# A scan and two mixture-of-experts layers: the first tile table in one run on VectorE

## The chip, the core and the metric

The kernel runs on one core of a Trainium2 chip. The metric is the time of the whole program in microseconds of the device; a run's profile also gives the span from the first to the last instruction. TensorE does the matrix products, VectorE and ScalarE the work on elements, GpSimd the writes to indexed rows, and SyncE and ScalarE issue most of the other transfers.

## The reference

The input is 2 sequences of 5056 tokens with 256 features. A gated scan along each sequence is followed by two layers that send each token to the one expert of eight with the highest logit:

```python
f = lower_bound + (1.0 - lower_bound) * sig        # sig = sigmoid(f_logit)
for t in range(S):
    h = f[:, t] * h + (1.0 - f[:, t]) * x[:, t]
    y[:, t] = h
# layer 1: logits = (y/|y|) @ (emb/|emb|).T / tau; layer 2: logits = x @ w_gate
expert_idx = argmax(logits)
out[mask] = gate_w[mask] * (relu(x[mask] @ w1[e]) @ w2[e])   # for each expert e
```

The 10112 tokens are 79 tiles of 128. w1 is 8 x 256 x 1024 and w2 8 x 1024 x 256 in each layer.

## The kernel before

**Products in half precision.** Each fp32 operand is split into a half-precision part and a remainder (hi and lo), and three products of the parts are summed. So each of the 64 weight blocks (512 KB: layer, w1 or w2, half h of the 1024 hidden features, expert e) is loaded, its hi part is written by ScalarE (`w_hi`, L410), and its lo part, the weight remainder, by VectorE (`w_lo`, L207). For four blocks of the first 16 (`wpe`, numbers 2, 6, 9 and 12) TensorE makes the remainder instead (`w_sub`, L447 and L448) and ScalarE copies it out (`w_sub2`, L456). L207, L211, L212 and L215 are helpers that many steps share.

**Names in rows.** W_0_102 and W_1_103 are the two halves of w1, W_0_104 and W_1_105 those of w2. The weights of the first half are made first; until they are needed, the second halves' memory holds raw weights and the first eight chunks of the input. `ws` is one of three other buffers for raw weights.

**Chunks and groups.** The scan goes over 40 chunks of 256 tokens (two tiles). A chunk is loaded (L488), gated (L495, L501), multiplied (the product, L521 through L207, which reads `xf` and writes `xf`), scanned (two L529), turned by TensorE into `yt` (L578, L580), squared (L595), scaled and split into a row (L618 and L207 `row`). Two chunks make a group q of four tiles: its best expert is found (`lg`, `mx`, `er`, `m`, `oh`), TensorE ranks its tokens among those of their expert (`rank_mm`, L466 and L468, which writes `RK`), VectorE reads the slots (`er<-RK`, `sl`), TensorE moves the counts up (`rank_up`, L473 and L475), and GpSimd puts the rows into the DRAM tensor X at their slots (`p_put`, L714), four transfers a group.

**Tables and units.** After groups 3 and 5 and others `checkpoint` reads the counts and writes a table (`ci`, `ct`, `le`, `tab`) of the tiles of one expert that are full; the first has 9 tiles. SyncE reads the table and loads such a tile turned (`xT`, L837); the load waits for all puts of the table's groups. A unit is one tile and one half h: 24 products with w1 into `hps` (L880), ScalarE's relu (L893), VectorE's remainder `hT<-hps` (L207), and three units later 12 products with w2 into `ops` (L912), which ScalarE copies out (L916). The first 8 tiles go through h = 0 as units 0 to 7 and through h = 1 as units 8 to 15. TensorE's six accumulator buffers are shared by `yt`, `wd`, `hps` and `ops`.

**What sets the order.** A plan gives each step a number and a rank in it; chunk c's steps count from `s0[c]`, which runs from -29 for the first chunk, and for chunk 8 jumps to `hold[1]`; from chunk 10 on `first` sets it. Up to step 17 only SyncE keeps the order of the plan: that of the other engines is made by a scheduler when the program is built, from the plan's priorities. `tc.issue_after(i)` holds instructions in that order behind instruction i.

Of the kernel before, what the change touches and what calls it, by code (L numbers as in the profile page):

```python
# [14 lines left out]
ALU = mybir.AluOpType  # L15
# [46 lines left out]
          'gat': (9, 54),  # L62
          'put': (10, 12),
          'cp': (10, 58)},
 'hold': (8, -9),
 'rates': ((17, 2), (99, 4)),
 'alias': 8,
 'mans': 17,
# [76 lines left out]
def scan_moe_moe_kernel(ctx, tc, xf, emb, cst, tmp, w1a, w2a, w1b, w2b, out, seq, cfg=CFG):  # L145
# [59 lines left out]
    def stt(eng, out, in0, s, in1, op0, op1, **kw):  # L205
        assert eng is V
        return eng.scalar_tensor_tensor(out=out, in0=in0, scalar=s, in1=in1, op0=op0, op1=op1, **kw)  # L207
# [15 lines left out]
    def ins_of(i):  # L223
        return getattr(i, "ins", i)
# [245 lines left out]
    def rank_up(m, oh, g):  # L470
        b = rkb[m][0]
        r = RK[:, b:b + g, :]
        T.matmul(out=r, lhsT=tri16b, rhs=oh[:, 0:g, :], start=False, stop=True, skip_group_check=True)  # L473
        for s in range(1, g):
            T.matmul(out=r[:, 0:g - s, :], lhsT=ones16, rhs=oh[:, s:g, :], start=False, stop=True, skip_group_check=True)  # L475


    ck = {}
    pq = {}
    prev = {}  # L480

    def p_load(c, eng=None):
        g = min(CT, NT - c * CT)
# [25 lines left out]
    def p_scan(c):  # L509
        d = ck[c]  # L510
        n, t = d["g"] * P, d["t"]
        f, y = t[:, 2:4, 0:n], t[:, 0:2, 0:n]
        if p_split(c):
            tt(G, y, f, y, ALU.mult)
            eng = cfg["y1"][c % len(cfg["y1"])]
            if eng == "A":
                A.activation(out=f, in_=f, func=ACTF.Copy, bias=1.0)
            else:
                ts(G if eng == "G" else V, f, f, 1.0, None, ALU.add)
        else:  # L520
            stt(V, y, f, 1.0, y, ALU.subtract, ALU.mult)  # L521
        yield
        a = c * TW
        cuts = [0] + [b - a for b in range(seq, N, seq) if a < b < a + n] + [n]
        for i in range(len(cuts) - 1):
            lo, hi = cuts[i], cuts[i + 1]
            for k in range(2):
                init = 0.0 if (a + lo) % seq == 0 else (t[:, k, lo - 1:lo] if lo else prev["y"][:, k])
                V.tensor_tensor_scan(out=t[:, k, lo:hi], data0=t[:, 2 + k, lo:hi], data1=t[:, k, lo:hi],  # L529
                                     initial=init, op0=ALU.mult, op1=ALU.subtract)  # L530
                yield
        prev["y"] = t[:, 0:2, n - 1:n]
# [157 lines left out]
        p["sl"] = sl  # L690

    def p_up(q):
        rank_up(0, pq[q]["oh"], pq[q]["g"])
        counted[0] += pq[q]["g"]

    def p_gat(q):
        p = pq[q]
        g, row = p["g"], p["row"]
        xv = row[:, :, 512:RW].bitcast(F32)
        G.tensor_copy(out=xv[:, 0:g, 1], in_=tok[:, q * G4:q * G4 + g])  # L700
        se = sm.tile([P, G4, 1], F32, name="se", tag="se")
        V.tensor_reduce(out=se[:, 0:g], in_=p["sh"][:, 0:g], axis=AX.X, op=ALU.add)
        yield
        stt(V, se[:, 0:g, 0], se[:, 0:g, 0], 1e-9, p["sc"][:, 0:g], ALU.add, ALU.mult)
        yield
        V.reciprocal(out=xv[:, 0:g, 0:1], in_=se[:, 0:g])
        yield

    def p_put(q, rows):
# [519 lines left out]
    def wstep(load, hi, lo, lo2):  # L1229
# [7 lines left out]
        if lo is not None:  # L1237
            t = wbuf.pop(lo)
            nlo[0] += 1
            i = nlo[0]  # L1240
            if i in cfg["wpe"]:
                wps[lo] = (w_sub(lo, t), t)
            elif 16 < i <= 32 and tablast:
                with behind(lo, V, tablast[0]):
                    w_lo(lo, t)
                w_done(lo)
            else:
                w_lo(lo, t)
                w_done(lo)
        if hi is not None:  # L1250
            with behind(hi, A):
# [275 lines left out]
```

## Time and profile before

| | us |
|---|---|
| median of 3 runs | 1048.29 (1043.24 to 1054.22) |
| the profiled execution | 1049.57 |
| its span | 1047.8 |
| TensorE busy in the span | 983.6 (94%) |
| VectorE, ScalarE, GpSimd busy | 780.0, 516.2, 428.2 |

The profile is one execution, so its times are compared with its own 1049.57 us, 1.8 us of which lie outside the span. Busy shares are means over the span: the first tenth, in which the scan and the weights are prepared, looks different from the rest.

### The profile page before, as it was taken

Reading aid. Unit: us, or ns where it says so; the run is one execution under the profiler, and the core shown is the slowest. Engines: PE = TensorE matmul, PEld = TensorE weight load, DVE = VectorE, ACT = ScalarE, POOL = GpSimd, SP = SyncE. Lnnn points to the kernel's source line nnn. Section 1 sums busy time; section 2 is a strip of 40 time slices with the busy share of each in tenths; the row PEclk is TensorE's granted clock in tenths of the full one; section 3 lists DMA queues with packets and bytes.
Section 4 is the critical chain, followed back from the end, with each engine's and each line's share of the span. In section 5 each row is a group of like instructions: output and inputs, shape, how many; then the busy total and the mean of one; then the engine's idle time right before and its main releaser. Section 6 shows DMA issues by size and latency. Waiting matters only on the chain.

```text
span 1047.8 us, 33840 instructions
## 1 busy us (share of the span) xinstructions
PE 983.6 (94%) x11795; PEld 859.2 (82%) x11795; DVE 780.0 (74%) x2288; ACT 516.2 (49%) x1266; POOL 428.2 (41%) x686
## 2 busy tenths in 40 slices
PE   5647999998999999999999999999999999999997
PEld 4436899897999899999999888998777777777775
DVE  7878797787888786765448877447777777777775
ACT  6867666555655554665345565443333333333332
POOL 5642447665666565432003550243222222222223
PEclk9967999999999999999999999999999999999999
DMA  9797545887888785965379699652222222221220
GB/s 355 244 328 170 158 93 136 155 163 135 166 161 157 141 150 104 203 200 147 60 181 208 112 212 245 116 104 72 52 52 52 52 52 51 46 52 45 47 47 31
DMA packets 216964, 137.64 MB, mean 131 GB/s; under 512 B 190961, under 2 KB 193918, under 8 KB 216800
## 3 DMA queue, kind: packets, MB, share of 16 engines
q1 hardware_dynamic: 192736, 61.63, 32.1%
q10 hardware_dynamic: 12208, 42.29, 14.7%
q0 software_dynamic: 11856, 31.51, 10.4%
q8 instruction: 105, 1.72, 0.7%
q14 instruction: 59, 0.48, 0.2%
HBM read 58.89 MB, written 38.85 MB: 93 GB/s over the span
## 4 chain that ended last, share of the span: by engine, by line
PE 49%; DMA 3%; DVE 2%; issue 1%; ACT 1%; POOL 0%; ACTq 0%; POOLq 0%
PE hps L869 10%; PE ops L908 10%; PE ops L912 9%; PE hps L880 9%; PE hps L870 5%; PE ops L909 5%; DMA X<-trow,tsl 2%; DMA xT<-X 1%; DVE hT L207 1%; DVE trow L207 0%; DVE W L207 0%; DVE trow L211 0%; PE x2p L978 0%; ACT hT L893 0%; ACT trow L935 0%
## 5 line engine op out<-in xcount | busy, mean ns | idle before, releaser
L880 PE MATMUL hps<-xT,W 128*128 128x128 f16 x4992 | 318.8, 220 | 15.3 <-DMA xT<-X 11.6
L880 PEld LDWEIGHTS <-W 128*128 x4992 | 299.0, 98 | 22.5 <-DMA xT<-X 11.8
L912 PE MATMUL ops<-W,hT 128*128 x2496 | 310.7, 274 | 3.3 <-ACT acc L916 2.7
L912 PEld LDWEIGHTS <-hT 128*128 128x128 f16 x2496 | 234.9, 98 | 31.2 <-issue 4.2
L891 DVE TENSOR_REDUCE acc<-hps 128x256 f32<-128x512 f32 x248 | 169.9, 687 | 63.5 <-PE hps L870 63.5
L207 DVE SCALAR_TENSOR_TENSOR hT<-hps,hT 128x512 f16<-128x512 f32 x208 | 142.0, 686 | 88.7 <-ACT hT L893 87.8
L1083 POOL DMA_INDIRECT out<-osum,ti x83 | 81.1, 977 | 268.7 <-DVE acc L891 227.3
L893 ACT ACTIVATE hT<-acc 128x512 f16<-128x512 f32 x124 | 78.1, 630 | 222.6 <-DVE acc L891 222.6
L893 ACT ACTIVATE hT<-hps 128x512 f16<-128x512 f32 x208 | 123.2, 592 | 116.5 <-PE hps L880 103.1
L869 PE MATMUL hps<-xT,W 128*128 128x256 f16 x992 | 177.1, 273 | 0.0
L870 PE MATMUL hps<-xT,W 128*128 128x128 f16 x992 | 170.4, 219 | 0.0
L908 PE MATMUL ops<-W,hT 128*128 x496 | 167.8, 379 | 0.0
L909 PE MATMUL ops<-W,hT 128*128 x496 | 135.2, 273 | 0.0
L1058 POOL DMA_INDIRECT X<-trow,tsl x83 | 91.8, 1106 | 67.9 <-issue 23.6
L869 PEld LDWEIGHTS <-W 128*128 x992 | 97.1, 98 | 24.1
L714 POOL DMA_INDIRECT X<-row,sl x79 | 90.3, 1143 | 57.3 <-ACT hT L893 19.4
L870 PEld LDWEIGHTS <-W 128*128 x992 | 97.1, 98 | 1.4
L207 DVE SCALAR_TENSOR_TENSOR hT<-acc,hT 128x512 f16<-128x512 f32 x124 | 84.5, 682 | 2.2 <-ACT hT L893 2.2
L908 PEld LDWEIGHTS <-hT 128*128 128x128 f16 x496 | 48.5, 98 | 45.6
L950 ACT ACTIVATE trow<-osum,tsc 128x256 f16<-128x256 f32 x62 | 28.2, 501 | 60.4 <-DVE tsc L212 57.1
L909 PEld LDWEIGHTS <-hT 128*128 128x128 f16 x496 | 48.5, 98 | 4.3
L207 DVE SCALAR_TENSOR_TENSOR W<-ws,W 128x1024 f16<-128x1024 f32 x35 | 42.6, 1221 | 11.8 <-ACT W L410 11.5
(170 smaller groups left out, 1297.1 us busy)
## 6 DMA issues: line engine op xcount, KB each, us to landing
xf<-xf ACTq DMA_DIRECT2D x27, 512.0 KB
ws<-w1b ACTq DMA_DIRECT2D x16, 512.0 KB
ws<-w2b ACTq DMA_DIRECT2D x16, 512.0 KB
W<-w1a SPq DMA_DIRECT2D x11, 512.0 KB
W<-xf SPq DMA_DIRECT2D x8, 512.0 KB
ws<-w2a ACTq DMA_DIRECT2D x8, 512.0 KB
WD<-wq SPq DMA_DIRECT2D x8, 512.0 KB
W<-WD ACTq DMA_DIRECT2D x8, 512.0 KB
```

Of the source, the lines that this page charges most:

```text
L207: return eng.scalar_tensor_tensor(out=out, in0=in0, scalar=s, in1=in1, op0=op0, op1=op1, **kw)
L714: w = G.indirect_dma_start(out=X[0], out_offset=IndirectOffsetOnAxis(ap=p["sl"][:, i, 0:1], axis=0), in_=p["row"][:, i, :].bitcast(I32), i ...
L869: T.matmul(out=hps[:, c % 2], lhsT=w[2 * k], rhs=xt[:, k:k + 3:2, :], start=(k == 0), stop=False)
L870: T.matmul(out=hps[:, c % 2, 0], lhsT=w[2 * k + 1], rhs=xt[:, k, :], start=False, stop=(k == 1))
L880: T.matmul(out=hps[:, c, :], lhsT=w, rhs=xt[:, a, :], start=(n == 0), stop=(n == 5))
L891: V.tensor_reduce(out=s[:, 2 * c:2 * c + 2].unsqueeze(3), in_=x.rearrange("p c b q -> p c q b"), axis=AX.X, op=ALU.add)
L893: i = A.activation(out=hh[:, 0], in_=hps, func=ACTF.Relu)
L908: T.matmul(out=t["o"].rearrange("p b d -> p (b d)"), lhsT=hT[:, k, :], rhs=w, start=(first and k == 0), stop=False)
L909: T.matmul(out=o, lhsT=hT[:, 4 + k, :], rhs=w[:, 0:D], start=False, stop=(last and k == 3))
L912: T.matmul(out=o, lhsT=hT[:, a + k, :], rhs=w[:, b * D:(b + 1) * D], start=(first and k == 0 and n == 0), stop=(last and k == 3 and n == 2))
L1058: x_write(1, G.indirect_dma_start(out=X[1], out_offset=IndirectOffsetOnAxis(ap=sl[:, i, 0:1], axis=0), in_=d["row"][:, i].bitcast(I32), in ...
L1083: i = ins_of(G.indirect_dma_start(out=out, out_offset=IndirectOffsetOnAxis(ap=ti, axis=0), in_=r, in_offset=None, bounds_check=N - 1, oob_ ...
```

## The change

Chunks 8 and 9 count their steps from two steps later (`hold`). Of the weight remainders made on VectorE, numbers 7 and 8 are held behind group 2's reciprocal (`gats[2]`) and those from 10 to 16 that VectorE makes behind the last operation of the first table (`tablast[0]`); the two that TensorE makes, 9 and 12, are held behind group 3's `rank_up` (`ups[3]`). Chunk 8's product is held behind the last operation of the first table. Each of these holds is between instructions of one engine. Nothing that is computed changes.

```diff
- 'hold': (8, -9),
+ 'hold': (8, -7),
@@ rank_up
         for s in range(1, g):
-            T.matmul(out=r[:, 0:g - s, :], lhsT=ones16, rhs=oh[:, s:g, :], start=False, stop=True, skip_group_check=True)
+            i = T.matmul(out=r[:, 0:g - s, :], lhsT=ones16, rhs=oh[:, s:g, :], start=False, stop=True, skip_group_check=True)
+        return ins_of(i)
@@ p_scan
-            stt(V, y, f, 1.0, y, ALU.subtract, ALU.mult)
+            with tc.issue_after(tablast[0]) if c == cfg["hold"][0] else ExitStack():
+                stt(V, y, f, 1.0, y, ALU.subtract, ALU.mult)
@@ p_up
-        rank_up(0, pq[q]["oh"], pq[q]["g"])
+        ups[q] = rank_up(0, pq[q]["oh"], pq[q]["g"])
@@ p_gat
-        V.reciprocal(out=xv[:, 0:g, 0:1], in_=se[:, 0:g])
+        gats[q] = ins_of(V.reciprocal(out=xv[:, 0:g, 0:1], in_=se[:, 0:g]))
@@ wstep
             if i in cfg["wpe"]:
-                wps[lo] = (w_sub(lo, t), t)
+                with tc.issue_after(ups[3]) if 3 in ups and i < 16 else ExitStack():
+                    wps[lo] = (w_sub(lo, t), t)
...
             else:
-                w_lo(lo, t)
+                with tc.issue_after(tablast[0] if tablast else gats[2]) if i > 6 else ExitStack():
+                    w_lo(lo, t)
                 w_done(lo)
```

The scheduler makes a new order out of this. On VectorE, the second half of the first table stood so before, with `xf` (chunk 10), `row` (chunk 8) and a weight remainder between its operations:

```order
L529 SCALAR_TENSOR_TENSOR xf<-xf 128x256 x2
L207 SCALAR_TENSOR_TENSOR ct<-ct,cs 128x8
L211 TENSOR_SCALAR ct<-ct 128x8
L212 TENSOR_SCALAR tab<-le 128x9
L207 SCALAR_TENSOR_TENSOR row<-yt,sc,row 128x256 x2
L215 TENSOR_TENSOR ct<-ct 128x7
L212 TENSOR_SCALAR ct<-ct 128x1
L215 TENSOR_TENSOR ct<-ct 128x8
L207 SCALAR_TENSOR_TENSOR W_0_104<-W_1_103,W_0_104 128x4x256
L215 TENSOR_TENSOR le<-le,ct 128x72
L215 TENSOR_TENSOR pt_112<-pt_112,ct 128x8
L212 TENSOR_SCALAR pi<-ss 128x2
```

and stands so now:

```order
L212 TENSOR_SCALAR tab<-le 128x9
L215 TENSOR_TENSOR ct<-ct 128x7
L212 TENSOR_SCALAR ct<-ct 128x1
L215 TENSOR_TENSOR ct<-ct 128x8
L215 TENSOR_TENSOR le<-le,ct 128x72
L215 TENSOR_TENSOR pt_112<-pt_112,ct 128x8
L782 TENSOR_REDUCE le<-le 128x9
L207 SCALAR_TENSOR_TENSOR le<-cs,le 128x9
L212 TENSOR_SCALAR tab<-le,ct 128x9
L207 SCALAR_TENSOR_TENSOR W_0_104<-W_1_103,W_0_104 128x4x256
L207 SCALAR_TENSOR_TENSOR xf<-xf 128x512
L207 SCALAR_TENSOR_TENSOR W_0_104<-W_1_103,W_0_104 128x4x256
```

The table's operations follow each other, and the remainders, with the products of chunks 8 and 10 among them, come behind the last `tab`.

Also on VectorE, behind the table, group 4's choice of expert (chunks 8 and 9; it ends with `oh`, which TensorE's rank of group 4 reads) stood so before:

```order
L212 TENSOR_SCALAR tab<-le,ct 128x9
L657 TENSOR_REDUCE m_765<-er 128x4
L215 TENSOR_TENSOR lg<-lg,ri 128x32
L215 TENSOR_TENSOR oh<-er,m_765 128x32
L207 SCALAR_TENSOR_TENSOR W_0_104<-ws,W_0_104 128x4x256
L215 TENSOR_TENSOR er<-RK,oh 128x32
L207 SCALAR_TENSOR_TENSOR xf<-xf 128x512
L207 SCALAR_TENSOR_TENSOR row<-yt,sc,row 128x256
L688 TENSOR_REDUCE sl<-er 128x4
L207 SCALAR_TENSOR_TENSOR row<-yt,sc,row 128x256
L702 TENSOR_REDUCE se<-lg 128x4
L529 SCALAR_TENSOR_TENSOR xf<-xf 128x256 x2
```

and now, with the end of the same choice in the last row:

```order
L207 SCALAR_TENSOR_TENSOR W_1_103<-W_1_105,W_1_103 128x2x512
L672 RECIPROCAL ri<-ri 128x4
L212 TENSOR_SCALAR sc<-pi 128x2
L215 TENSOR_TENSOR lg<-lg,mx 128x32
L207 SCALAR_TENSOR_TENSOR W_0_104<-ws,W_0_104 128x4x256
L207 SCALAR_TENSOR_TENSOR row<-yt,sc,row 128x256 x2
L207 SCALAR_TENSOR_TENSOR er<-lg,cs 128x32
L207 SCALAR_TENSOR_TENSOR W_1_103<-W_1_105,W_1_103 128x2x512
L207 SCALAR_TENSOR_TENSOR row<-yt,sc,row 128x256 x2
L660 TENSOR_REDUCE m_783<-er 128x4
L215 TENSOR_TENSOR lg<-lg,ri 128x32
L215 TENSOR_TENSOR oh<-er,m_783 128x32
```

The last three remainders of w2's first half (`W_0_104<-ws`), the first two of w1's second half (`W_1_103`), chunk 11's product and its scans now stand ahead of `oh`; before they stood behind it.

On TensorE, group 3's rank (L466, `RK<-oh`) stood so before, behind the remainder products of block 9 (`wd<-W_0_104`) and chunk 8's turn (`yt<-cs,xf`):

```order
L447 MATMUL wd<-W_1_103,cs 128x512
L448 LDWEIGHTS idn
L448 MATMUL wd<-W_0_104,idn 128x512
L447 MATMUL wd<-W_1_103,cs 128x512
L448 LDWEIGHTS idn
L448 MATMUL wd<-W_0_104,idn 128x512
L578 MATMUL yt<-cs,xf 128x128 x2
L580 MATMUL yt<-cs,xf 128x8 x2
L578 MATMUL yt<-cs,xf 128x128 x2
L580 MATMUL yt<-cs,xf 128x8 x2
L466 LDWEIGHTS tri_107
L466 MATMUL RK<-oh,tri_107 128x32
```

and now, directly behind those of block 6 (`wd<-W_0_102`):

```order
L448 MATMUL wd<-W_0_102,idn 128x512
L466 LDWEIGHTS tri_107
L466 MATMUL RK<-oh,tri_107 128x32
L468 LDWEIGHTS ones_109
L468 MATMUL RK<-oh,ones_109 128x24
L468 LDWEIGHTS ones_109
L468 MATMUL RK<-oh,ones_109 128x16
L468 LDWEIGHTS ones_109
L468 MATMUL RK<-oh,ones_109 128x8
L473 LDWEIGHTS tri16b
L473 MATMUL RK<-oh,tri16b 128x32
L475 LDWEIGHTS ones_109
```

The products of blocks 9 and 12, chunks 8's and 9's turns and group 4's rank and count follow; group 4's count is still the last before the first unit's L880, as it was before.

## Rows read from the trace of the kernel before

**Rows 1.** Windows view: length, busy us of PE, PEld, DVE, ACT, POOL, clock, DMA share, GB/s.
```profile
80.00:88.00 8.00, 3.78 (x41) 3.06 (x39) 6.83 (x8) 8.00 (x16) 3.00 (x4) 0.91 0.95 146
88.00:95.00 7.00, 6.44 (x44) 6.00 (x45) 6.15 (x10) 4.55 (x12) 0.00 (x0) 0.50 0.56 125
...
140.00:200.00 60.00, 57.16 (x814) 53.76 (x813) 49.72 (x220) 38.50 (x121) 39.01 (x68) 1.00 0.63 127
```

**Rows 2.** Timeline of TensorE: start, length, instruction, [idle before it <- what ended it].
```profile
52.08 0.18 PE L466 MATMUL RK<-oh,tri 128*128 128x32 f16 x1
...
66.91 0.19 PE L466 MATMUL RK<-oh,tri 128*128 128x32 f16 x1 [3.06 <-DVE oh L215]
...
73.15 5.92 PE L880 MATMUL hps<-xT,W 128*128 128x128 f16 x72 [4.76 <-DMA xT<-X]
...
82.28 1.59 PE L912 MATMUL ops<-W,hT 128*128 x12
88.56 2.74 PE L880 MATMUL hps<-xT,W 128*128 128x128 f16 x24 [4.70 <-DMA xT<-X]
...
100.31 2.72 PE L912 MATMUL ops<-W,hT 128*128 x12 [2.47 <-ACT acc L916]
```

**Rows 3.** Timeline of VectorE: the first table.
```profile
49.25 0.18 DVE L215 TENSOR_TENSOR oh<-er,m 128x32 f16<-128x32 f32 x1
...
54.61 0.17 DVE L207 SCALAR_TENSOR_TENSOR ci<-RK,cs 128x8 int32<-128x8 f32 x1
...
55.48 0.17 DVE L760 TENSOR_TENSOR_SCAN ct<-ct 128x8 f32<-128x8 f32 x1
55.69 0.17 DVE L215 TENSOR_TENSOR ct<-ct 128x8 f32<-128x8 f32 x1
55.78 0.23 DVE L215 TENSOR_TENSOR le<-ct,cs 128x72 f32<-128x72 f32 x1
...
63.37 1.23 DVE L207 SCALAR_TENSOR_TENSOR W<-W,W 128x1024 f16<-128x1024 f32 x1 [3.96 <-ACT W L410]
64.51 0.23 DVE L215 TENSOR_TENSOR le<-le,ct 128x72 f32<-128x72 f32 x1
...
66.31 0.23 DVE L212 TENSOR_SCALAR tab<-le,ct 128x9 int32<-128x9 f32 x1
...
66.66 0.19 DVE L215 TENSOR_TENSOR oh<-er,m 128x32 f16<-128x32 f32 x1
```

**Rows 4.** Timeline of VectorE: chunks 8 and 9 ahead of the table.
```profile
37.94 0.68 DVE L207 SCALAR_TENSOR_TENSOR xf<-xf 128x512 f32<-128x512 f32 x1
38.55 0.17 DVE L215 TENSOR_TENSOR er<-RK,oh 128x32 f32<-128x32 f32 x1
38.66 1.39 DVE L529 TENSOR_TENSOR_SCAN xf<-xf,W 128x256 f32<-128x256 f32 x2
...
40.04 1.65 DVE L207 SCALAR_TENSOR_TENSOR row<-yt,sc,row 128x256 f16<-128x256 f32 x4
...
45.11 0.17 DVE L706 RECIPROCAL row<-se 128x4 f32<-128x4 f32 x1
...
52.64 0.18 DVE L669 RECIPROCAL ri<-ri 128x4 f32<-128x4 f32 x1 [1.26 <-POOL ri L211]
```

**Rows 5.** Timeline of GpSimd: first put of group 2 and of group 4.
```profile
46.06 1.19 POOL L714 DMA_INDIRECT X<-row,sl  x1 [4.58 <-ACT W L456]
...
73.66 2.93 POOL L714 DMA_INDIRECT X<-row,sl  x1 [7.60 <-DVE row L706]
```

**Rows 6.** Timeline of SyncE: the fifth load of a tile.
```profile
81.17 1.25 SPq L837 DMA_TRANSPOSE xT<-X  x1
```

**Rows 7.** Timeline of ScalarE, its queue of DMA issues (ACTq) included.
```profile
90.42 0.63 ACT L495 ACTIVATE xf<-xf 128x512 f32<-128x512 f32 x1 [1.67 <-DMA xf<-xf]
...
93.66 0.33 ACTq L397 DMA_DIRECT2D ws<-w2a  x1
...
97.26 1.06 ACT L410 ACTIVATE W<-ws 128x1024 f16<-128x1024 f32 x1 [1.92 <-DMA ws<-w2a]
```

More of the change, by code (lines that the diff above doesn't have):

```diff
@@ L480, in scan_moe_moe_kernel @@
     prev = {}
+    ups, gats = {}, {}
     def p_load(c, eng=None):
```

## The prediction

> **What bounds the kernel now.** I read the windows view first. [...] TensorE's timeline, read next, names the waits: 4.76 us for the first loaded tile, to 73.15; 4.70 for the fifth, to 88.56; 2.47 for ScalarE's copy `acc`, to 100.31 [rows 2]. The reader is to see that the first matmul of the layer waits for a transfer, and that this transfer follows the table. VectorE's timeline, third, shows why the table is late: it starts at 54.61, stops for 3.96 us because a remainder in its midst waits for ScalarE's hi part, and ends at 66.31 [rows 3].
>
> So the table is on the path to 73.15. But TensorE keeps a fixed order, and group 4's rank and count stand ahead of the first unit before and after the change. That decides the case: an early table helps the first unit only if group 4's one-hot `oh` comes early too.
>
> **Part 1, the table starts earlier.** Ahead of the table VectorE loses chunk 8's product (37.94 to 38.55, 0.61), chunk 8's scans (38.66 to 40.04, 1.38 with one small operation, say 1.3) and chunk 9's, 1.3 [rows 4]. One remainder (1.14, from 63.37 to 64.51 [rows 3]) changes places with group 2's reciprocal at 45.11 [rows 4]. The reciprocal so comes 0.61 + 1.3 + 1.3 + 1.14 = 4.3 us earlier, at about 41. Group 2's puts, first at 46.06 [rows 5], start near 42, GpSimd is free for group 3's `ri` 4 us earlier, and VectorE's wait of 1.26 for it at 52.64 [rows 4] goes. On TensorE group 3's rank, at 52.08 behind two blocks' remainder products and chunk 8's turn, needs `oh` alone, which starts at 49.25 [rows 2, 3]; it can run at 49.5. The table's first operation then comes at about 50.0 instead of 54.61. Bounds: 49.3 if the work ahead of it moves too (a `wd` product follows the rows of 40.04, which now start 1.5 earlier), 51.5 if GpSimd or ScalarE's exponential holds it.
>
> **Part 2, the table in one run.** In the new order 24 operations stand from `ci` to the last `tab`. Where one waits for the one ahead, starts are 0.21 apart (55.48 to 55.69); where it doesn't, 0.09 (55.69 to 55.78) [rows 3]. I count nine pairs with no other operation to fill the gap: 9 x 0.21 + 15 x 0.09 = 3.2 us; bounds 24 x 0.09 = 2.2 and 24 x 0.21 = 5.0. I take 3.2, since the pairs are counted. The table ends at 53.2 instead of 66.5, 13 us earlier.
>
> [...]
>
> **Part 3, from the table to the first unit.** Remainders, products and scans went behind the table, and the new order puts most of them ahead of group 4's `oh`. Between the last `tab` and that `oh` stand: 8 remainders (six of w2's first half, two of w1's second), 8 x 1.14 = 9.1; products of chunks 8, 10 and 11, 3 x 0.61 = 1.8; scans of four chunks, 4 x 1.3 = 5.2; four rows of group 4, 1.65 as at 40.04 [rows 4]; eleven small operations, 1.1. The sum is 18.9 us, and the list is dense: nothing in it can overlap, since it is one engine. `oh` ends at 53.2 + 18.9 = 72.1. Then rank, slots and count: 66.66 to 66.91 for `oh` to rank [rows 2, 3], two more such steps, together 1.0. The first unit starts at 73.1, where it starts at 73.15 before. The 13 us of the table are spent on VectorE's moved work, and the first matmul gains nothing. What hides the early load of tiles is this work; what was late by transfer is now late by `oh`. The transfer wait of 4.76 becomes a wait for VectorE. The earlier loads don't collide with much: the weights stand ahead of them in SyncE's own queue.
>
> **Part 4, behind the first unit.** Here something is gained, because five pieces that VectorE did behind `oh` are done. The fifth tile's load is issued at 81.17 [rows 6]; before it SyncE's queue had to pass four loads that waited for transfers of raw weights, whose buffers the late remainders hold. Now those remainders end before 70, and the fifth load needs only unit 0's buffer, free at about 76 (the row of 5.92 at 73.15 holds units 0 to 2, 1.97 each [rows 2]; 73.1 + 2.0 = 75.1, and 0.9 put on for the queue). From its issue at 81.17 to the start at 88.56 it took 7.4 us [rows 2, 6], so it lands at 76 + 7.4 = 83.4 at the latest. TensorE gets to unit 4 at 73.1 + (82.28 + 1.59 - 73.15) = 83.8 [rows 2]. The wait of 4.70 goes, and unit 4 starts 88.56 - 83.8 = 4.8 us earlier.
>
> It is not 4.7 at the end, since the accumulators are late next. ScalarE's order from there to 100 is the same: relus, hi parts, chunk 13 and 14, then the copy `acc` that frees the accumulator for 100.31. Of its waits, that for chunk 14's load (1.67, to 90.42 [rows 7]) stays: this load takes its buffer from group 4's rows, and group 4's puts start at 73.66 [rows 5] with the first unit, as before. The load of raw weights at 93.66 waited for TensorE's turn of chunk 11, which follows unit 4; it can now go out right behind chunk 14's gate, at about 91, 2.5 us earlier, and the hi part at 97.26, that waits 1.92 for it [rows 7], with it. If group 4's puts find the queues emptier (the first took 2.93 us, the first of group 2 1.19 [rows 5]), up to 1.7 more goes. So 100.31 moves by 2.5 to 4.2; I take 3.3, the middle, since the puts may gain or not. TensorE idles instead between 86 and 97, so its clock falls there as it did from 88 to 95; the product at 100.31 already took 2.72, where that at 82.28 took 1.59 [rows 2], so this isn't a new cost.
>
> **The sum.** 0 for the first unit, -3.3 at 100.31, 0 behind it: 1049.57 - 3.3 = 1046.3 for an execution like the profiled one. That lies 1.3 above the median of the three runs, so the median becomes 1048.29 - 3.3 = 1045.0.
>
> **The rivals.**
> Nothing gained: chunk 14's load keeps ScalarE to 90.42 and the raw weights land no sooner, because the tiles' transfers share the engines with them. For it: ScalarE is busy 8.00 of 8 us from 80 to 88 [rows 1] and its order is unchanged. Against: TensorE's turn of chunk 11 does move. Time 1048.3, give or take 1. A change that doesn't do what it says (the table held in its midst by ScalarE's exponential) ends here too, as the first unit waits for `oh` in any case.
>
> All stalls go: 4.2 idle from 80 to 88, 2.47 at 100.31, and half of 6.44 at the half clock from 88 to 95 [rows 1, 2] are 9.9 us: 1038.4. It needs accumulators freed 5 us earlier than ScalarE's order allows.
>
> [...]
>
> Slower: VectorE holds 8.4 us more ahead of `oh` than before, in a fixed order, so one remainder that waits for its weights delays the first unit in full, as the remainder at 63.37 delayed the table by 3.96 [rows 3]. With that wait and a table 1.5 late (the bound of part 1), the first unit starts at 73.1 + 5.5 = 78.6, and puts, chunk 14 and relus follow: 1045.0 + 5.5 = 1050.5. It decides from a delay of 3.3 on. Against: the remainders' order follows that of the loads, and most of them were late before because of VectorE, not of a transfer; how far each load is ahead, no row here says.
>
> **How the numbers follow.** The forecast 0.42, nothing gained 0.25, slower 0.15, all stalls gone 0.10, semaphores free 0.08. Predicted is the likeliest, 1045.0. The range 1039 to 1051.5 leaves out half of "all stalls gone" and the worse part of "slower". The three runs shown lie 1.0% apart, so one per cent, 10.5 us, is about what can be told from no change. Only the far end of "all stalls gone" is faster by that (0.06), and only two late remainders in "slower" are slower by it (0.03); the rest, 0.91, is within.
>
> **What the profile after would show.** The last `tab` near 53 and no wait among the table's rows; tiles loaded by 70; TensorE's wait before the first L880 put down to VectorE's `oh`, with L880 at 73 (72 to 75); unit 4 near 84 with no wait for `xT`; waits for ScalarE or VectorE between 86 and 97; `ops` near 97 where 100.31 stood. I am wrong if the first unit starts before 71 (the list of part 3 isn't dense) or after 76 (a remainder waits), or if later stretches don't carry the shift.

## The result and the profile after

| | before | after |
|---|---|---|
| median, us | 1049.11 (20 runs) | 1058.21 (20 runs) |
| ratio | | 1.0069, interval 1.0046 to 1.0092 |
| span of the profiled execution | 1047.8 | 1056.3 |

Slower by 0.7%, some 7.2 us (4.8 to 9.7). Forecast were 3.3 us less. The ratio compares the fast runs alone and is not that of the two medians, which is 1.0087.

First the stretch that the prediction spoke of. VectorE's timeline after, from `ci` to group 4's `oh` (compare [rows 3]):

```profile
49.72 0.17 DVE L207 SCALAR_TENSOR_TENSOR ci<-RK,cs 128x8 int32<-128x8 f32 x1
...
50.53 0.17 DVE L763 TENSOR_TENSOR_SCAN ct<-ct 128x8 f32<-128x8 f32 x1
50.74 0.17 DVE L215 TENSOR_TENSOR ct<-ct 128x8 f32<-128x8 f32 x1
...
52.47 0.23 DVE L212 TENSOR_SCALAR tab<-le,ct 128x9 int32<-128x9 f32 x1
...
72.36 0.19 DVE L215 TENSOR_TENSOR oh<-er,m 128x32 f16<-128x32 f32 x1
```

The table now stands in one run of 2.9 us, 14 us earlier, and `oh` starts 19.9 us behind its last row. All of this was forecast (50.0, 53.2, 72.1). TensorE's timeline after, same columns as [rows 2]:

```profile
72.61 0.18 PE L466 MATMUL RK<-oh,tri 128*128 128x32 f16 x1 [11.29 <-DVE oh L215]
...
75.23 6.67 PE L883 MATMUL hps<-xT,W 128*128 128x128 f16 x72 [1.84 <-DMA xT<-X]
...
85.84 2.00 PE L883 MATMUL hps<-xT,W 128*128 128x128 f16 x24
...
90.28 0.44 PE L581 MATMUL yt<-cs,xf 128*128 128x128 f32 x2 [1.57 <-ACT acc L919]
...
93.12 2.72 PE L915 MATMUL ops<-W,hT 128*128 x12 [2.06 <-DVE hT L207]
...
100.00 2.72 PE L915 MATMUL ops<-W,hT 128*128 x12 [2.58 <-ACT acc L919]
```

L883 is L880 of before and L915 is L912: the diff shifts lines by 3. The rank waits for `oh` as forecast, the fifth tile (85.84) waits for nothing. But the first unit starts at 75.23, not 73.1, and its last wait is for a transfer. SyncE's waits from 40 to 95 us after (line, what it waited for, us in total, times, longest), and its first load of a tile, from its timeline:

```profile
SPq L840 <- DMA ws<-w2a: 7.6, 2, 6.3
```
```profile
66.43 1.31 SPq L840 DMA_TRANSPOSE xT<-X  x1
```

and the same load before:

```profile
68.07 1.31 SPq L837 DMA_TRANSPOSE xT<-X  x1
```

The table is there at 52.7, yet the first load of a tile is issued at 66.43: it stands in SyncE's queue behind the raw weights, and its own wait is put down to a load of them (`ws<-w2a`, 6.3 us). So 14 us of table bought 1.6 us of load. And from that issue to the first unit 8.8 us pass, where before it was 5.1.

The third product with w2, at 100.31 before and forecast near 97, comes at 100.00, again behind a wait for `acc` (2.58 us). ScalarE's timeline after, with the gate of chunk 14, the load of raw weights behind it and that `acc` (compare [rows 7]):

```profile
92.50 0.63 ACT L497 ACTIVATE xf<-xf 128x512 f32<-128x512 f32 x1 [2.28 <-DMA xf<-xf]
...
93.23 0.33 ACTq L397 DMA_DIRECT2D ws<-w2a  x1
...
99.57 0.38 ACT L919 ACTIVATE acc<-ops 128x256 f32<-128x256 f32 x1
```

The gate waits until 92.50 (90.42 before) for a load that was issued at 84.00 (84.08 before), so the raw weights go out at 93.23 and not at 91, and `acc` is at 99.57 (99.88 before).

So far the forecast gain is missing, but nothing accounts for a span that is 8.5 us longer. The second place lies 370 us further on, at the branch behind layer 1's tiles, where the prediction expected nothing. TensorE's timeline after:

```profile
468.10 1.50 PE L883 MATMUL hps<-xT,W 128*128 128x128 f16 x24
473.37 1.01 PE L981 MATMUL x2p<-id,trow 128*128 128x128 f16 x8 [3.77 <-PEq L1385]
474.17 2.77 PE L915 MATMUL ops<-W,hT 128*128 x12
...
476.83 2.29 PE L883 MATMUL hps<-xT,W 128*128 128x128 f16 x24
478.95 1.47 PE L915 MATMUL ops<-W,hT 128*128 x12
```

The same place before:

```profile
464.53 0.61 PE L978 MATMUL x2p<-id,trow 128*128 128x128 f16 x8 [0.30 <-PEq L1380]
464.98 1.47 PE L912 MATMUL ops<-W,hT 128*128 x12
...
466.34 1.50 PE L880 MATMUL hps<-xT,W 128*128 128x128 f16 x24
```

TensorE does the same work, but its own sequencer (PEq) holds it for 3.77 us at the branch, not 0.30: the view of that line's instructions has TensorE's branch at 4.17 us, and at 0.42 before. The branch goes past code for further tiles, which neither execution runs. The next three groups run longer, 1.01 for 0.61, 2.77 for 1.47, 2.29 for 1.50, and the windows view grants a clock of 0.54 from 473 to 479 us after, and 1.00 from 464 to 470 before. The sum of the differences is 3.47 + 0.40 + 1.30 + 0.79 = 6.0 us. On the page's list of DMA queues one line differs by one packet: instructions, 106 packets and 1.74 MB after, 105 and 1.72 MB before, so a packet is 16 KB of code. In the built programs TensorE has 11,799 instructions ahead of that branch before and 11,800 after. In sum one separate wait for a semaphore is added.

The third place is between them. Moments of one step in several profiles show it best: starts of TensorE's units and products with w2, and ScalarE's k-th relu (`hT<-hps`). The means are over the four profiles with before's order (before, f1, f2, h4) and the six with the changed order (after, f3, f4, h1, h2, i2) in which before's own median was 1049 to 1055 us (all runs are below):

| step | before's order, us (least to most) | changed order, us | difference |
|---|---|---|---|
| fifth unit | 86.6 (85.4 to 88.6) | 84.6 (82.9 to 85.8) | -2.0 |
| 2nd product with w2 | 92.1 (91.1 to 93.4) | 92.2 (91.0 to 93.1) | +0.1 |
| 3rd product with w2 | 98.3 (97.0 to 100.3) | 97.8 (96.7 to 100.0) | -0.5 |
| 7th relu | 103.6 (102.6 to 105.6) | 101.4 (100.6 to 104.3) | -2.2 |
| 8th relu | 109.6 (108.4 to 112.0) | 110.7 (109.7 to 114.4) | +1.1 |
| 13th relu | 127.0 (125.8 to 129.1) | 130.1 (128.3 to 132.3) | +3.2 |
| 24th relu | 166.7 (165.5 to 169.0) | 170.4 (168.0 to 173.2) | +3.7 |

The fifth unit's gain is gone by the second product with w2. (The 7th relu is early only on ScalarE: the changed order has it ahead of a hi part behind which it stood before.) From the third product to the 13th relu 3.6 us are lost.

### The profile page after: what moved, and what is told of

Its sections match the earlier page's. It is cut to its first block, busy times and chain, and to the rows that moved or that the text cites. A ratio compares the mean times of both kernels' runs of the same rounds, so it can differ in the third digit from the quotient of the medians.

```text
span 1056.3 us, 33842 instructions
## 1 busy us (share of the span) xinstructions
PE 986.0 (93%) x11795; PEld 860.4 (81%) x11795; DVE 781.4 (74%) x2288; ACT 517.4 (49%) x1266; POOL 422.9 (40%) x686
## 3 DMA queue, kind: packets, MB, share of 16 engines
q8 instruction: 106, 1.74, 0.7%
## 5 line engine op out<-in xcount | busy, mean ns | idle before, releaser
L883 PE MATMUL hps<-xT,W 128*128 128x128 f16 x4992 | 319.8, 221 | 6.1 <-DMA xT<-X 3.3
L915 PE MATMUL ops<-W,hT 128*128 x2496 | 313.1, 275 | 5.3 <-ACT acc L919 2.6
L883 PEld LDWEIGHTS <-W 128*128 x4992 | 300.1, 99 | 13.4 <-issue 3.8
L915 PEld LDWEIGHTS <-hT 128*128 128x128 f16 x2496 | 236.0, 99 | 33.5 <-issue 5.9
L873 PE MATMUL hps<-xT,W 128*128 128x128 f16 x992 | 170.4, 219 | 0.0
L912 PE MATMUL ops<-W,hT 128*128 x496 | 135.2, 273 | 0.0
L717 POOL DMA_INDIRECT X<-row,sl x79 | 88.1, 1116 | 55.2 <-ACT hT L896 21.9
L912 PEld LDWEIGHTS <-hT 128*128 128x128 f16 x496 | 48.5, 98 | 4.2
```

The costliest lines, as they stand in the source:

```text
L717: w = G.indirect_dma_start(out=X[0], out_offset=IndirectOffsetOnAxis(ap=p["sl"][:, i, 0:1], axis=0), in_=p["row"][:, i, :].bitcast(I32), i ...
L873: T.matmul(out=hps[:, c % 2, 0], lhsT=w[2 * k + 1], rhs=xt[:, k, :], start=False, stop=(k == 1))
L883: T.matmul(out=hps[:, c, :], lhsT=w, rhs=xt[:, a, :], start=(n == 0), stop=(n == 5))
L912: T.matmul(out=o, lhsT=hT[:, 4 + k, :], rhs=w[:, 0:D], start=False, stop=(last and k == 3))
L915: T.matmul(out=o, lhsT=hT[:, a + k, :], rhs=w[:, b * D:(b + 1) * D], start=(first and k == 0 and n == 0), stop=(last and k == 3 and n == 2))
```

## The experiments

Ratios are to the kernel before as run beside the experiment on the same chip. The quoted expectations were on record before the runs.

### Which part of the change

**e1_acc_first**: the changed kernel, with chunk 15's gate on ScalarE held behind the fourth copy `acc`.

```diff
-        A.activation(out=f, in_=f, func=ACTF.Tanh, scale=0.5)
+        with tc.issue_after(accs[3]) if c == 15 else ExitStack():
+            A.activation(out=f, in_=f, func=ACTF.Tanh, scale=0.5)
...
```

> The changed kernel, with one more hold on ScalarE: the gate of chunk 15 behind the copy `acc` of the fourth unit, as the order of before has it (the changed kernel has the gate, which waits 3.16 us for its load until 112.03, ahead of the copy, and TensorE then waits 2.29 us for that copy, to 116.08). Theory A, the later order: the scheduler's new order of the steps after 100 us is the loss; the twentieth relu then comes at 154 to 155.5 instead of 157.6, and the median falls from about 1058 to 1053 to 1055. Theory B, the transfers: the loss comes from the first unit, which starts at 75.2 instead of 73.2 since raw weights land ahead of its tile; this kernel changes nothing there, and stays at 1056 to 1059.

**e2_no_prod**: the changed kernel without the hold on chunk 8's product.

```diff
-            with tc.issue_after(tablast[0]) if c == cfg["hold"][0] else ExitStack():
-                stt(V, y, f, 1.0, y, ALU.subtract, ALU.mult)
+            stt(V, y, f, 1.0, y, ALU.subtract, ALU.mult)
```

> The changed kernel without the hold of chunk 8's product; the holds of the remainders and the two later steps stay. Chunk 8's scan comes early again, so the last raw load of the second half of w1 is again early in ScalarE's queue, and about 5 us of VectorE's work leaves the list ahead of group 4's `oh`. Theory B: the first loaded tile lands at 73 or earlier and the first unit starts at 71 to 73; time 1048 to 1051. Theory A: ScalarE has the copy `acc` ahead of chunk 15's gate here, so the twentieth relu is at 154 to 155; but VectorE's order of the second table is a new one, so 1049 to 1053. Theory C, that VectorE's list ahead of `oh` alone sets the first unit: `oh` at 62 to 65 and the first unit at 65 to 67, 1041 to 1044.

**e3_no_prod_no_steps**: e2, and chunks 8 and 9 at their old steps (`'hold': (8, -9)`); of the change only the holds on remainders are left.

> The changed kernel without the hold of chunk 8's product and with chunks 8 and 9 at their steps of before; only the remainders are held. The table stands in one run here too, and the order of the engines behind 100 us is nearly that of before. Theory A: at least as good as before, 1044 to 1049, and better than the kernel with the later steps by 2 to 4 us. Theory B: the first unit at 71 to 73, 1045 to 1049, and the same as the kernel with the later steps. Theory C: the first unit at 65 to 67, 1040 to 1043.

**e4_steps_only**: the kernel before with `'hold': (8, -7)` alone.

> The kernel before with chunks 8 and 9 two steps later and no hold at all. Two remainders and chunk 8's scans stand again ahead of the table, so the first table ends late, at 60 to 66. Theory A: the order behind 100 us is the new one of the later steps, so 1050 to 1054. Theory B: the load order on ScalarE is that of before, so the first unit is at 73 and the time that of before, 1047 to 1050.

| | ratio | interval | last `tab` | first unit | wait at the branch |
|---|---|---|---|---|---|
| e1 | 1.0104 | 1.0053 to 1.0154 | 52.23 | 73.25 | 4.5 |
| e2 | 1.0042 | 1.0003 to 1.0081 | 54.65 | 73.89 | 0.3 |
| e3 | 1.0032 | 1.0003 to 1.0062 | 54.86 | 72.49 | 0.3 |
| e4 | 1.0120 | 1.0075 to 1.0165 | 59.73 | 71.64 | 4.1 |

My first theory, that ScalarE's order (its gates ahead of the copies `acc`) is what costs, fell: e1 is no faster than the changed kernel. Nor is it chunk 8's product ahead of `oh`: without it (e2, e3) the ratio is still above 1, if barely. What sorts the four is not in the stretch that was edited. The two with a wait of over 4 us at the branch have the highest ratios, and e4 the highest of all though its first unit comes earliest. That made the branch the next theory.

### The place of the code

The edit writes TensorE's first matmul, which fills `RK`, several times; it adds instructions to TensorE and moves nothing on any other engine.

```diff
-        T.matmul(out=RK, lhsT=ones16, rhs=s0, start=True, stop=True, skip_group_check=True)
+        for _ in range(N):
+            T.matmul(out=RK, lhsT=ones16, rhs=s0, start=True, stop=True, skip_group_check=True)
```

**f1_before_again** and **f3_after_again** are the two kernels unchanged; **f2_before_2more** is before with N = 2 (two instructions more, a weight load and a product), **f4_after_98more** after with N = 50.

> The kernel before once more, unchanged, for a profile on the same chip as the other three of this call. All theories: ratio 1.000. Theory D, the place of the code: the built program has 11799 TensorE instructions ahead of the branch behind the first layer, and there is no long wait of TensorE's sequencer there (0.3 us, as in the first profile), between the relus 123 and 125.

> The kernel before, with the first matmul of the program (it sets the counts to their start values, in a time in which TensorE idles for 5 us) done twice: two TensorE instructions more, 11801 ahead of the branch, and no other change on any engine. Theory D: the target of that branch now lies in another block of code, as in the three kernels with 11800 instructions (the changed kernel and two experiments), whose traces have one packet of code more and a wait of 3.8 to 4.5 us at the branch: this one gets it too, and is 5 to 6 us slower than before, a ratio of 1.005 to 1.006. Theories A and B (order behind 100 us, transfers of the first tile): 1.000, since nothing that they speak of changes.

> The changed kernel once more, unchanged, on the chip of the others. Ratio 1.005 to 1.009 as measured. Theory D: the wait of 3.5 to 4.5 us at the branch is there again, and 5 to 6 us of the distance to before are made between the relus 123 and 125. Theories A and B: the distance is made by relu 24 (4 us) and the wait at the branch is chance, gone in this execution.

> The changed kernel with the same first matmul done 50 times: 98 TensorE instructions more, in TensorE's idle time at the start (they take some 3 of 5 us there), and no other change on any engine; 11898 instructions ahead of the branch. Theory D: where the branch and its target now lie to the block bounds isn't known; if the bad places are few, the wait at the branch goes and the kernel is 5 to 6 us faster than the changed one, a ratio of 1.000 to 1.002 to before; if it stays, the ratio is that of the changed kernel, and the bad places span at least 98 instructions. Theories A and B: that of the changed kernel.

Measured: f1 1.0018 (0.9982 to 1.0053), f2 1.0066 (1.0030 to 1.0103), f3 1.0073 (1.0040 to 1.0106), f4 1.0020 (0.9988 to 1.0051). TensorE's timeline at the branch in f2:

```profile
466.71 1.01 PE L979 MATMUL x2p<-id,trow 128*128 128x128 f16 x8 [4.01 <-PEq L1381]
467.52 2.76 PE L913 MATMUL ops<-W,hT 128*128 x12
```

and in f4:

```profile
465.45 0.61 PE L982 MATMUL x2p<-id,trow 128*128 128x128 f16 x8 [0.30 <-PEq L1386]
465.90 1.47 PE L916 MATMUL ops<-W,hT 128*128 x12
```

Two harmless instructions make the kernel before as slow as the changed one, and 98 take most of the loss from the changed one. This cost belongs to where the code lies, not to what it does.

**h1_after_1fewer** approaches the same from the other side: the changed kernel with the wait for chunk 0's load put where an instruction already waits, so that TensorE has 11,799 instructions again; the order on each engine stays. **h2_after_hint_later** leaves 11,800 and moves the program's hint for this branch from 813 to 184 instructions ahead of it. **h4_before_third** is before.

```diff
-            T.transpose(pe[:, k, :], em[:, k * P:(k + 1) * P], idt[0:E, 0:E])
+            i = T.transpose(pe[:, k, :], em[:, k * P:(k + 1) * P], idt[0:E, 0:E])
+        tc.add_manual_dep(ins_of(i), ck[0]["ld"].name, ...)
...
```

> The changed kernel with one TensorE instruction fewer: the second turn of the embedding at the start also waits for the load of chunk 0, so that the separate instruction with that wait ahead of chunk 0's first turn goes; 11799 instructions ahead of the branch, as in the kernel before, and the order of every engine is that of the changed kernel. Theory D, the place of the code: no wait of TensorE's sequencer at the branch (0.3 us), and the distance to before shrinks from 1.007 to 0.999 to 1.003. Theories A and B, the order behind 100 us and the transfers of the first tile: 1.005 to 1.009, since nothing of that is changed.

> The changed kernel, with the instruction that announces the branch to TensorE's sequencer moved from 813 instructions ahead of the branch to 184 ahead; 11800 instructions as in the changed kernel, nothing else moves. If the announced block of code is no longer held when the branch comes 813 instructions later (in the places that are bad): the wait is gone, 0.999 to 1.003. If the announcement plays no part in it: the wait stays, 1.005 to 1.009.

> The kernel before once more, for a profile on the chip of these runs: ratio 1.000; no wait at the branch; its first unit at 72 to 74.

h1 1.0049 (1.0019 to 1.0078) with a wait of 0.3, h2 1.0092 (1.0058 to 1.0126) with 4.0, h4 0.9986 (0.9953 to 1.0019) with 0.3. Moving the hint leaves the wait as it was; one instruction takes it away. But h1 stays above 1, so the place isn't all.

**g2_before_98more** and **g3_before_50more** are before with N = 50 and N = 26; **g1_after_order_98more** and **h3_after_order_1fewer** are the changed kernel with N = 50 and two holds on ScalarE (chunk 15's gate behind the fourth `acc`, chunk 16's behind the eighth relu); both are the same kernel, run on two chips.

> The changed kernel with 98 TensorE instructions more at its start (so without the wait at the branch, as the experiment before), and with two holds on ScalarE that give it the order of before behind 100 us: the gate of chunk 15 behind the fourth copy `acc`, and the gate of chunk 16 behind the eighth relu. Theory A, now for what is left: the new order behind 100 us takes back what the first units gain; with the old order the twentieth relu, at 153.1 in the last run, comes 1.5 to 2.5 us earlier, and the ratio to before is 0.997 to 1.000. Against it: the second table's order on VectorE stays new, or the times of the first units differ from execution to execution by as much; then 1.001 to 1.003, as without the holds.

> The kernel before with its first matmul done 50 times: 98 TensorE instructions more, 11897 ahead of the branch, no other change. Theory D: the added matmuls lie in idle time, and the branch and its target are where those of the changed kernel with 98 more are, without a wait; ratio 0.999 to 1.001. If the 98 cost something themselves (3 us at the start are on the path), 1.002 to 1.003.

> The kernel before with its first matmul done 26 times: 50 TensorE instructions more, 11849 ahead of the branch. Theory D says that the wait at the branch hangs on where the code lies, and leaves open how many places are bad: two instructions more gave it, 98 more didn't. If bad is a stretch of places (the target has gone over a bound of a block, the branch not yet): the wait of 4 us is here too, and the ratio 1.005 to 1.007. If bad are only a few places at one bound: no wait, and 0.999 to 1.001.

> The changed kernel with the two holds on ScalarE that give it the order of before behind 100 us; 98 TensorE instructions more, as in the run of the other chip (ratio 1.0059 there, with a wait of 1.6 us at the branch in its profile). Theory A for what is left: better than the changed kernel with one instruction fewer by 1 to 3 us. Without it: the same, 1.000 to 1.004.

g1 1.0059 (1.0028 to 1.0090), h3 1.0025 (0.9991 to 1.0059), g2 1.0044 (1.0011 to 1.0076), g3 1.0035 (0.9996 to 1.0073). Instructions are no free remedy: beside g2, 98 more cost the kernel before 0.4% though its wait at the branch is 0.3. That holding ScalarE's gates brings back what h1 lacks is not shown: g1 and h3 lie on both sides of h1. TensorE's timeline of g2 shows where part of the 98's cost lies, in the unit right behind the branch:

```profile
483.99 0.49 PE L881 MATMUL hps<-xT,W 128*128 128x128 f16 x6
486.01 1.18 PE L881 MATMUL hps<-xT,W 128*128 128x128 f16 x18 [1.52 <-issue]
```

TensorE stops for 1.52 us and waits for nothing that the profile shows. All four kernels with 98 more have such a stop (1.2 to 1.5 us): behind the 6th product of that unit with 11,897 instructions, behind the 5th with 11,898. So the stop stays at a place of the code, and the cost at the branch has in part moved there. The wait at the branch, and the time from the 120th to the 123rd relu, which holds the branch and the unit behind it, against TensorE's instructions ahead of the branch, over all kernels:

| instructions | kernels | wait, us | 120th to 123rd relu, us |
|---|---|---|---|
| 11,795 to 11,799 | before, f1, h4, e2, e3, h1, i1, i2 | 0.3 | 8.8 to 9.2 |
| 11,800 | after, f3, h2, e1, e4, g4 | 3.8 to 4.5 | 14.3 to 15.5 |
| 11,801 | f2 | 4.0 | 15.3 |
| 11,849 | g3 | 2.4 | 12.5 |
| 11,897, 11,898 | g2, f4, h3, g1 | 0.3, 0.3, 0.4, 1.6 | 11.8, 10.5, 10.9, 13.0 |

The rows show a wait at the branch that comes between 11,799 and 11,800 instructions and is small again 98 further on. The one packet of code more (106 for 105) is not by itself the wait: f4, g2 and h3 move 106 too, with 0.3 to 0.4 us at the branch. With 11,800 instructions the wait is 3.5 to 4.2 us longer, and the slower groups behind it add 1.4 (h2) to 2.6 (g4). What in the place of the code brings the wait is not shown.

### The first unit

**g4_before_fewer_bytes**: the kernel before; of two raw w1 blocks ahead of the first tile only 256 of 1024 columns are loaded.

```diff
-        hwq().dma_start(out=t, in_=wsrc[m][which][:, h, e, :])
+        n = 256 if item in ((0, 0, 1, 1), (0, 0, 1, 2)) else 1024
+        hwq().dma_start(out=t[:, 0:n], in_=wsrc[m][which][:, h, e, 0:n])
```

> The kernel before, with a quarter of the bytes in two of the raw loads of the second half of w1 that stand in SyncE's queue just ahead of the first tile (384 KB each left out; three quarters of two weight blocks are then not the weights). Theory B, the transfers: the first tile waits for bytes and not for the table, so its first unit starts 1.5 to 2.5 us earlier than the 72.4 and 73.2 of before, at 70 to 71.5, though the table is no earlier. Against it (the table and `oh` set it): at 72 to 73.5. The built program has 11800 TensorE instructions ahead of the branch, so it also has the wait there; its time says nothing else.

In its one execution the first unit starts at 71.51, where two kernels with before's order have 72.87 and 74.04 on the same chip (g2, g3). 0.8 MB less bring it 1.4 to 2.5 us forward, with the table at 65.26. The windows of 55 to 73 us fit that (before, then after; columns as in [rows 1], the last two the DMA share and GB/s):

```profile
55.00:73.00 18.00, 7.37 (x26) 4.31 (x26) 13.21 (x48) 12.07 (x25) 6.21 (x7) 0.52 1.04 342
```
```profile
55.00:73.00 18.00, 6.56 (x34) 3.98 (x34) 16.66 (x34) 13.68 (x31) 3.87 (x5) 0.60 1.06 341
```

The DMA share is 1.04 and 1.06, at 342 and 341 GB/s; VectorE's busy time is what moved, from 13.21 to 16.66 us.

### The order from 102 to 130 us

In the six profiles with the changed order GpSimd does group 6's `ri` behind group 5's four puts, and ScalarE's exponential waits for it. **i1_after_1fewer_ri_first** is h1 with `ri` moved back ahead of those puts; **i2_after_1fewer_again** is h1 beside it.

```diff
+            with tc.issue_after(ris[6]) if q == 5 else ExitStack():
                 w = G.indirect_dma_start(out=X[0], ...)
...
-                        at(b + j, prio, p_put, q, (j,))
+                        at(b + j + (q == 5), prio, p_put, q, (j,))
```

> The changed kernel with one TensorE instruction fewer ahead of the branch (as in the run of that kind before) and, on GpSimd, the two `ri` operations of group 6 ahead of group 5's four puts, as the kernel before had them; the orders of TensorE and SyncE are the changed kernel's, on VectorE and ScalarE group 6's later steps follow `ri` and come earlier. Theory of the order: in all five profiles with the changed order ScalarE's exponential behind that `ri` waits 1.4 to 2.4 us at 121 to 126 us, and the load of the next chunk is issued behind it, some 3 to 4 us later than in the four of before, where it waits 0.16; with `ri` ahead the wait falls to under 0.3, the 13th relu (128 to 132 us with the changed order, 126 to 127 before in like executions) comes at 124 to 126, and the time is 3 to 4 us below the run beside it: ratio to the kernel before 0.997 to 1.002. Rival, the late `ri` is only a sign: TensorE or a transfer holds the relus in any case; the wait goes but the relu stays at 128 to 130 and the ratio at 1.003 to 1.006. TensorE's wait at the branch 0.3 in both.

> The changed kernel with one TensorE instruction fewer ahead of the branch, unchanged otherwise, run beside the one with `ri` first. Both theories: the wait at the branch 0.3, the exponential's wait about 2, the 13th relu at 128 to 131, ratio 1.002 to 1.008. If the ratio comes out at 1.000 or below, the cost of the order was the spread of the earlier measurement, and the code's place alone is left.

i1 1.0007 (0.9971 to 1.0043), i2 1.0022 (0.9985 to 1.0059): the two can't be told apart. ScalarE's timeline tells more. Before (h4):

```profile
117.21 0.23 ACT L676 ACTIVATE lg<-lg 128x32 f32<-128x32 f32 x1 [0.16 <-DVE lg L215]
...
118.24 0.33 ACTq L488 DMA_DIRECT2D xf<-xf  x1
...
123.14 0.63 ACT L495 ACTIVATE xf<-xf 128x512 f32<-128x512 f32 x1 [1.49 <-DMA xf<-xf]
123.67 0.58 ACT L893 ACTIVATE hT<-hps 128x512 f16<-128x512 f32 x1
```

The changed order (i2):

```profile
121.32 0.23 ACT L680 ACTIVATE lg<-lg 128x32 f32<-128x32 f32 x1 [2.34 <-DVE lg L215]
...
123.85 0.33 ACTq L491 DMA_DIRECT2D xf<-xf  x1
...
127.48 0.63 ACT L498 ACTIVATE xf<-xf 128x512 f32<-128x512 f32 x1 [1.23 <-DMA xf<-xf]
128.01 0.58 ACT L897 ACTIVATE hT<-hps 128x512 f16<-128x512 f32 x1
```

With `ri` first (i1):

```profile
121.17 0.23 ACT L680 ACTIVATE lg<-lg 128x32 f32<-128x32 f32 x1
...
127.47 0.34 ACTq L491 DMA_DIRECT2D xf<-xf  x1
...
131.86 0.63 ACT L498 ACTIVATE xf<-xf 128x512 f32<-128x512 f32 x1 [1.98 <-DMA xf<-xf]
132.39 0.58 ACT L898 ACTIVATE hT<-hps 128x512 f16<-128x512 f32 x1
```

The rows are the exponential (`lg<-lg`), the issue of chunk 17's load (`xf<-xf` on ACTq), its gate, and the relu behind the gate in ScalarE's order. In i1 the exponential waits no longer, and the load is issued no earlier for it: the late `ri` is only a sign, as the rival said. (That execution was 4 us late already at 105.) What the load follows is GpSimd. The fourth put of group 5 starts at 118.77 in h4, 118.22 in i2 and 123.08 in i1:

```profile
118.77 0.98 POOL L714 DMA_INDIRECT X<-row,sl  x1 [0.30 <-issue]
```
```profile
118.22 0.97 POOL L718 DMA_INDIRECT X<-row,sl  x1 [0.30 <-issue]
```
```profile
123.08 0.98 POOL L719 DMA_INDIRECT X<-row,sl  x1 [0.30 <-issue]
```

In the four profiles with before's order the load goes out 0.4 to 0.5 us ahead of that put, in seven of the changed order (the six and i1) 3.4 to 5.6 behind it. The built programs give a reason. The listing of ScalarE's instructions with their waits has, before and after:

```
210 L488 DMA xf<-xf 128x1024
207 L490 DMA xf<-xf 128x1024 [waits DMASW6_49,DMASW7_49,DMASW1_49,DMAHW4_49,DMASW0_49,Pool_49]
```

Chunks (`xf`, L489) and the groups' rows (`row`, L594) share one set of buffers. In the new order chunk 17 gets a buffer for which it waits for GpSimd's puts (DMASW is their queue); before it got one that needed no wait. Its load goes out 4.2 us later (mean 123.8 over six, 119.6 over four), its gate 3.2 us later (127.5, 124.3), and the 13th relu 3.2.

## Why the prediction was wrong

**Table, list and `oh`** (parts 1 to 3): right. The table's first operation came at 49.72 (50.0), its 24 operations took 2.9 us (3.2), between the bound of 2.2, all starts 0.09 apart, and the counted pairs: the dependent start at 50.74 is 0.21 behind the one ahead of it, as in [rows 3]. From the last `tab` to `oh` 19.9 us passed (18.9), with a single wait of 1.18, for ScalarE. That the 13 us of the table buy the first unit nothing was the prediction's central step, and it held; the unit even starts 2.1 us later, and 1.4 in the mean.

**"What was late by transfer is now late by `oh`"** (part 3): half right. Both hold it now, the rank for `oh`, then the unit for 1.84 us more for its tile; its mean start over the four and six profiles is 72.9 and 74.3. "The earlier loads don't collide with much" was the wrong sentence: the stretch was full of raw weights (DMA share 1.04 and 1.06 from 55 to 73 us), the tile's load was issued behind them, and 8.8 us passed from its issue to the unit instead of 5.1.

**Behind the first unit** (part 4, -3.3 at 100.31): this step failed, and with it the whole gain. 100.31 became 100.00, 0.3 us instead of 3.3, and 0.5 in the mean; "`ops` near 97" did not come. The fifth tile's wait of 4.70 did go, but its unit came 2.7 us earlier and not 4.8, 2.0 in the mean: f1 and h4 have no such wait for the fifth tile, only one of 1.49 and 1.65 for the fourth, so much of the 4.70 was that one execution's chance. f1's fourth and fifth unit:

```profile
81.06 1.97 PE L880 MATMUL hps<-xT,W 128*128 128x128 f16 x24 [1.49 <-DMA xT<-X]
...
85.41 1.94 PE L880 MATMUL hps<-xT,W 128*128 128x128 f16 x24
```

The gain ended at the next product with w2 (+0.1). ScalarE frees the accumulators and was no earlier: after, it works from 78.0 to 90.2 without a wait, and its first four relus and first `acc` are 0.5 us later in the mean; TensorE waits for that `acc` at 90.28 (1.57). In the profiled pair the forecast that its wait for chunk 14's load ends at 90.42 failed too: it ended at 92.50, and the raw weights, forecast for 91, went out at 93.23.

**"0 behind it"** (the sum): this term failed as well, twice. From 100 to 130 us the new order loses 3.6 (-0.5 to +3.2). That chunk 17's load then waits for puts is shown by the programs' waits and by rows of every profile; that this alone is the cost is argued, since no run changed the buffer alone, and the two that changed what stands near it (ScalarE's gates, `ri`) measured no gain that stands clear of their intervals. And the branch costs 6.0 us by rows; by f2 against f1 beside it 0.48% (5 us), by the mean of the changed order with the wait (after, f3, h2: 1.0078) and without it (h1, i2, f4: 1.0030) 0.48% (5 us). What is left of the change itself is 0.3%, some 3 us; two of those three intervals reach 1. So about two thirds of the loss come from one instruction's place and one third from the order; the intervals allow some 2 to 8 us for the first.

That a shift made by 100 us reaches the end unchanged, as the 0 takes for granted, no run shows. The profiled pair is 11.3 us apart at the 126th relu and 8.7 at the 208th; h1 and i2, the same kernel on two chips, are 0.2 us apart at the 126th and 12.6 at the 208th.

**The rivals.** The slower one, with 0.15, had the sign and nearly the size for another reason: no remainder delayed `oh` by 5.5 us. "Nothing gained", with 0.25, described everything up to 100 us better than the forecast did, and by its own reasons: ScalarE has no time to spare (8.00 busy of 8 us [rows 1]), and chunk 14's load lands no sooner. For "semaphores free", with 0.08, no run speaks: after, the 24 operations took 2.9 us and not 2.2, and the dependent start at 50.74 came 0.21 us behind the one ahead, not 0.09. I gave no chance to a loss far from the edit: "if later stretches don't carry the shift" stood among the ways to be wrong, without a price.

No version beat the kernel before; the nearest, i1, is at 1.0007. Left open are whether another buffer for chunk 17 would keep the load early, and what makes up the rest of the 0.4% (some 4.7 us) that 98 more instructions cost before (g2), of which 2.6 lie between the 120th and the 123rd relu (11.8 for 9.2).

## What to carry to other kernels

When two builds differ by under one per cent, read the rows in which an engine waits for its own sequencer (here 0.30 us before, 3.77 after) before explaining the difference by the edit: a control kernel with one harmless instruction more or less tells the two apart. An order that a scheduler makes from priorities also hands out the buffers, so list, for the next few loads behind the edit, which releases they wait for, and not only the operations that moved. Size a wait from more than one execution where it stands on transfers: the one of 4.70 us, from which the forecast took its gain, was not there in the next two. And before counting a wait as a gain, look for the engine that frees the next buffer: here ScalarE, without a wait from 78.0 to 90.2 us, and a fifth unit 2.0 us earlier left the next product with w2 at +0.1.

## What the runs showed of the hardware

- One instruction more on TensorE, ahead of a taken branch 470 us into the program, costs 5 to 6 us (6.0 by rows in the profiled pair, 5 by f2, with two more, against f1): 0.3 us of wait at 11,799 instructions, 3.8 to 4.5 at 11,800. With 98 more the wait is 0.3 to 1.6, and TensorE stops for 1.2 to 1.5 us a few products behind the branch.
- The kernel before has medians from 1049 to 1067 us in the different sets of runs, far more than any ratio here; the chip alone does not explain it, since chip 12 has 1066.8 in one set and 1055.3 in another. So ratios were taken within one set.
- Executions of before's order differ by 3.3 us by the 13th relu (125.8 to 129.1 over three sets of runs), as much as the whole forecast gain.
